# Transposing the second LayerNorm's output by DMA instead of on TensorE in a diffusion transformer block

## Chip, cores and metric

The kernel runs on one core of a Trainium2 chip. The metric is the device time of one execution in microseconds (us). Times inside a trace count from the start of the profiled span, which is about 2 us shorter than the device time. The start of a span scatters by some tenths of a microsecond from run to run, so moments are compared between traces only where the difference is larger than that.

PE is TensorE and PEld its weight load, DVE is VectorE, ACT is ScalarE, POOL is GpSimd. SP issues the loads. ACTq and SPq mark DMA issues on the queues of ACT and SP.

## The reference

One transformer block with adaptive modulation, cut to what matters. There are 512 tokens (B=2, N=256), D=1152, F=4608; all tensors are bfloat16.

```python
mod = (_silu(c) @ w_mod).reshape(B, 6, 1, D)
shift_a, scale_a, gate_a, shift_m, scale_m, gate_m = [mod[:, i] for i in range(6)]
# ... first LayerNorm, qkv, attention with 2 heads ...
x  = x + gate_a * (attention_output @ wo)
h2 = _layernorm(x, axis=-1) * (1 + scale_m) + shift_m     # the part that is changed
m  = _gelu(h2 @ w_fc1) @ w_fc2
return x + gate_m * m
```

## The kernel before

The program is written as a list of units with declared reads and writes. A scheduler orders DVE, ACT and POOL; PE and SP keep the order of the program text. Every wait is a semaphore wait worked out from the reads and writes.

The tokens are handled in four tiles of 128 (t = 0 to 3). For each tile `wo_tile` multiplies by `wo`, adds the residual, and normalises into `XN2[t]`, tokens on the partitions. fc1 needs features on the partitions, so each tile is transposed. Before, PE did that in nine 128x128 pieces into PSUM, and DVE and ACT applied the modulation (scale and shift) while they copied PSUM to `H2T`:

```python
def xn2_T(t):
    ...
    for kt in range(KT):                                  # KT = 9
        tr(slot[kt], xn2[:, kt * 128:(kt + 1) * 128], IDENT)          # PE, into PSUM
    for kt in range(KT):                                  # modulation, PSUM -> H2T
        if kt < (4 if t < 2 else 6): dve(...)             # tensor_scalar, mult and add
        else:                        act(...)             # activation Identity, scale and bias
```

fc1 has 36 output tiles of 128 features. The first F0 of them run in two halves of 256 tokens, so that they can start on token tiles 0 and 1 before 2 and 3 are ready; the others take all 512 tokens. fc1's weights come in nine blocks of 1.18 MB, each for four output tiles, through four buffers: block 4 (for tiles 16 to 19) reuses the buffer of block 0. fc2's weights come in four parts of 2.65 MB. Part 3 lies over the memory of `XN2`, so it has to wait for the last transpose. All these loads are issued by SP, in the order of the text:

```python
# ... wfc1_load(0) to (3) ...
for q4 in range(3):
    dma(WFC2[...], ...)                        # fc2 parts 0, 1, 2: early, ahead of attention's PV
# ... pv(b, h) ...
wo_tile(0); wo_tile(1); wo_tile(2)
xn2_T(0)
wo_tile(3, {2: lambda: xn2_T(1)})              # transposes of tile 1 ahead of the last wo chunk
for f in range(0, 4):        fc1_tile(f, 0, 256)
xn2_T(2)
for f in range(4, F0 - 2):   fc1_tile(f, 0, 256)      # F0 = 8
xn2_T(3)
for f in range(F0 - 2, F0):  fc1_tile(f, 0, 256)
dma(WFC2[:, 27:36, :], ...)                    # fc2 part 3
for f in range(F0):          fc1_tile(f, 256, 256)
for f in range(F0, JT):                        # JT = 36
    if f % 4 == 0 and f // 4 >= 4: wfc1_load(f // 4)
    fc1_tile(f, 0, 512)
# ... fc2, gate, residual, output ...
```

## Time and profile before

| | before |
|---|---|
| device time, median | 249.41 us (249.25 to 249.88) |
| PE busy | 98% of a span of 247.4 us |
| granted TensorE clock | 1.00 throughout |
| start of fc1 tile 16 | about 135.1 us (explained below) |

From the page of the kernel before: the first line gives busy time, share of the span and number of instructions; the rest cut the span into 40 slices of 6.2 us, with PE's busy share and clock in tenths and the DMA rate in GB/s.

```profile
PE 241.7 (98%) x1827; PEld 149.5 (60%) x1827; DVE 69.9 (28%) x179; ACT 63.8 (26%) x129; POOL 19.6 (8%) x33
...
PE   6999999999999999999999999999999999999995
...
PEclk9999999999999999999999999999999999999999
...
GB/s 240 372 375 393 390 299 414 426 423 420 409 385 332 309 364 391 392 386 383 358 156 138 191 191 3 0 0 0 3 16 16 19 16 16 16 19 21 27 19 17
```

PE is the bottleneck and hardly waits. The DMA engines move 299 GB/s or more in slices 2 to 20 and then have less and less to do.

The next lines are PE's part of the timeline of the kernel before: start, duration, engine, line, operation, output and input, count. L681 is the transposes, L678 all other matmuls. Durations overlap a little, because a matmul's end lies after the start of the next.

```profile
96.98 0.67 PE L681 MATMUL psum<-arena 128*128 128x128 bf16 x9
97.48 3.09 PE L678 MATMUL psum<-arena 128*128 128x384 bf16 x18
100.41 0.93 PE L681 MATMUL psum<-arena 128*128 128x128 bf16 x9
101.17 5.55 PE L678 MATMUL psum<-arena 128*128 128x384 bf16 x45
106.56 0.67 PE L681 MATMUL psum<-arena 128*128 128x128 bf16 x9
107.06 2.13 PE L678 MATMUL psum<-arena 128*128 128x256 bf16 x18
109.03 0.74 PE L681 MATMUL psum<-arena 128*128 128x128 bf16 x9
109.60 2.56 PE L678 MATMUL psum<-arena 128*128 128x256 bf16 x22
```

The four transpose groups hold PE from 96.98 to 97.48, 100.41 to 101.17, 106.56 to 107.06 and 109.03 to 109.60: 2.33 us together. That is all that the change can take from PE.

A gelu (L1059) on ACT's timeline of the kernel before tells when an fc1 tile is done. The first whole-width tile is tile 8 (gelu at 121.57), and they follow every 1.944 us.

```profile
135.17 0.60 ACT L1059 ACTIVATE arena<-psum 128x512 bf16<-128x512 f32 x1 [1.34 <-PE psum L678]
```

The gelu at 135.17 is that of tile 15, so PE began tile 16 at about 135.1. What follows it (20 fc1 tiles, fc2, output) takes 112.3 us.

The table by stretches of the kernel before gives, for each stretch, the busy time of each engine, then the granted clock, the DMA engines' busy share and GB/s.

```profile
core 0: us, PE busy (x) PEld busy (x) DVE busy (x) ACT busy (x) POOL busy (x), PEclk, DMA share, GB/s
...
96.00:100.00 4.00, 4.00 (x33) 2.64 (x31) 3.62 (x11) 2.32 (x4) 2.33 (x3) 1.00 1.05 390
100.00:104.00 4.00, 3.91 (x35) 2.83 (x34) 3.88 (x13) 3.45 (x9) 2.72 (x4) 1.00 1.06 392
...
```

While the normalisation and the transposes run, the queue moves fc2's weights at 390 to 392 GB/s.

### The profile page before, as it was taken

Reading aid. Unit: us, or ns where it says so; the run is one execution under the profiler, and the core shown is the slowest. Engines: PE = TensorE matmul, PEld = TensorE weight load, DVE = VectorE, ACT = ScalarE, POOL = GpSimd, SP = SyncE. Lnnn points to the kernel's source line nnn. Section 1 sums busy time; section 2 is a strip of 40 time slices with the busy share of each in tenths; the row PEclk is TensorE's granted clock in tenths of the full one; section 3 lists DMA queues with packets and bytes.
Section 4 is the critical chain, followed back from the end, with each engine's and each line's share of the span. In section 5 each row is a group of like instructions: output and inputs, shape, how many; then the busy total and the mean of one; then the engine's idle time right before and its main releaser. Section 6 shows DMA issues by size and latency. Waiting matters only on the chain.

```text
span 247.4 us, 4146 instructions
## 1 busy us (share of the span) xinstructions
PE 241.7 (98%) x1827; PEld 149.5 (60%) x1827; DVE 69.9 (28%) x179; ACT 63.8 (26%) x129; POOL 19.6 (8%) x33
## 2 busy tenths in 40 slices
PE   6999999999999999999999999999999999999995
PEld 2589954566656766798544444444566666666674
DVE  3742440555322679950000000000012222111112
ACT  4730340344301404984333222332000000000000
POOL 1300000000013167500000000000000000000000
PEclk9999999999999999999999999999999999999999
DMA  6999989999999999999953660000000000000000
GB/s 240 372 375 393 390 299 414 426 423 420 409 385 332 309 364 391 392 386 383 358 156 138 191 191 3 0 0 0 3 16 16 19 16 16 16 19 21 27 19 17
DMA packets 27644, 51.59 MB, mean 209 GB/s; under 512 B 1511, under 2 KB 15591, under 8 KB 26475
## 3 DMA queue, kind: packets, MB, share of 16 engines
q1 hardware_dynamic: 27216, 50.14, 56.0%
q0 software_dynamic: 384, 1.19, 1.5%
q8 instruction: 14, 0.23, 0.4%
q14 instruction: 3, 0.02, 0.0%
q10 hardware_dynamic: 27, 0.00, 0.0%
HBM read 50.14 MB, written 1.19 MB: 208 GB/s over the span
## 4 chain that ended last, share of the span: by engine, by line
PE 94%; ACT 2%; DMA 2%; DVE 1%; issue 0%
PE psum L678 92%; PE psum L681 2%; DMA arena<-in_x_dram 2%; ACT arena L1049 1%; ACT arena L1033 1%; ACT arena L731 1%; ACT arena L730 1%; DVE arena L744 0%; DVE arena L783 0%; DVE arena L1139 0%; DVE arena L732 0%; DVE arena L1140 0%; DVE arena L774 0%; DVE arena L734 0%
## 5 line engine op out<-in xcount | busy, mean ns | idle before, releaser
L678 PE MATMUL psum<-arena 128*128 128x384 bf16 (+7 forms) x1720 | 237.7, 305 | 1.8 <-POOL arena L701 1.4
L678 PEld LDWEIGHTS psum<-arena 128*128 128x128 bf16 (+1 forms) x1720 | 143.8, 97 | 91.0 <-issue 3.1
L1139 DVE TENSOR_TENSOR arena<-psum,arena 128x384 f32<-128x384 f32 (+3 forms) x14 | 7.0, 501 | 119.2 <-PE psum L678 119.2
L1059 ACT ACTIVATE arena<-psum 128x512 bf16<-128x512 f32 (+1 forms) x44 | 22.5, 522 | 42.6 <-PE psum L678 42.6
L673 ACT ACTIVATE arena<-psum 128x512 bf16<-128x512 f32 (+7 forms) x29 | 15.4, 553 | 36.2 <-PE psum L678 33.8
L675 DVE CAST arena<-psum 128x512 bf16<-128x512 f32 (+4 forms) x23 | 14.0, 621 | 32.1 <-PE psum L678 32.0
L1028 POOL TENSOR_TENSOR arena<-arena 128x384 f32<-128x384 f32 x12 | 11.0, 913 | 11.2 <-DVE arena L1027 10.0
L722 DVE BATCH_NORM_STATS2 arena<-arena 128x6 f32<-128x384 f32 (+1 forms) x18 | 9.5, 548 | 0.8 <-DMA arena<-in_x_dram 0.7
L681 PE MATMUL psum<-arena 128*128 128x128 bf16 (+2 forms) x107 | 7.8, 209 | 0.9 <-DMA arena<-in_c_dram 0.7
L681 PEld LDWEIGHTS psum<-arena 128*128 128x128 bf16 (+2 forms) x107 | 6.3, 97 | 3.7 <-DMA arena<-in_c_dram 1.6
L1033 ACT ACTIVATE arena<-arena 128x1152 bf16<-128x1152 f32 x4 | 5.4, 1353 | 9.5 <-DVE arena L1032 9.5
L1027 DVE TENSOR_TENSOR arena<-psum,arena 128x384 f32<-128x384 f32 x12 | 6.6, 548 | 3.2 <-PE psum L678 2.6
L1140 DVE TENSOR_TENSOR arena<-arena 128x384 bf16<-128x384 f32 (+3 forms) x14 | 7.0, 501 | 0.5
L1049 ACT ACTIVATE arena<-psum,arena 128x128 bf16<-128x128 bf16 x16 | 6.1, 460 | 3.2 <-PE psum L681 2.5
L659 POOL DMA_DIRECT2D dit_scratch<-arena x2 | 1.2, 629 | 61.3 <-DVE arena L675 61.3
L1046 DVE TENSOR_SCALAR arena<-psum,arena 128x128 bf16<-128x128 bf16 x20 | 5.5, 338 | 2.0 <-PE psum L681 1.8
L924 ACT ACTIVATE arena<-psum,arena 128x256 bf16<-128x256 f32 x8 | 3.7, 471 | 6.9 <-PE psum L678 5.4
L726 POOL TENSOR_TENSOR arena<-arena 128x1 f32<-128x1 f32 x6 | 3.3, 553 | 8.7 <-DVE arena L725 8.7
L887 ACT ACTIVATE arena<-arena 128x256 bf16<-128x256 bf16 x6 | 2.5, 496 | 4.3 <-DVE arena L881 4.3
L920 DVE TENSOR_REDUCE arena<-psum 128x2 f32<-128x512 f32 x4 | 2.8, 690 | 1.5 <-PE psum L678 1.5
L783 DVE TENSOR_SCALAR arena<-psum,arena 128x256 bf16<-128x256 bf16 x7 | 2.4, 349 | 2.7 <-PE psum L681 1.4
L928 DVE TENSOR_TENSOR arena<-arena 128x512 bf16<-128x512 bf16 x4 | 2.8, 688 | 0.1
(37 smaller groups left out, 30.9 us busy)
## 6 DMA issues: line engine op xcount, KB each, us to landing
arena<-in_w_mod_dram SPq DMA_DIRECT2D x3, 3456.0 KB, 25.9
arena<-in_w_fc_dram SPq DMA_DIRECT2D x9, 1152.0 KB, 8.6
arena<-in_w_fc_dram SPq DMA_DIRECT2D x4, 2592.0 KB, 20.7
arena<-in_wqkv_dram SPq DMA_DIRECT2D x18, 288.0 KB, 10.0
arena<-in_w_mod_dram SPq DMA_DIRECT2D x3, 864.0 KB, 13.1
arena<-in_wqkv_dram SPq DMA_DIRECT2D x1, 2592.0 KB, 10.0
arena<-in_wo_dram SPq DMA_DIRECT2D x1, 2592.0 KB, 39.7
arena<-in_w_mod_dram SPq DMA_DIRECT2D x3, 480.0 KB, 6.8
```

The costliest lines, as they stand in the source:

```text
L673: act(c_act(n), lambda e: e.activation(out=dst, in_=src, func=ACTF.Copy), [src], [dst], name)
L675: dve(c_dve_psum16(n) if psum16 else c_dve_psum32(n), lambda e: e.tensor_copy(dst, src), [src], [dst], name)
L678: S.instr(lambda e: e.matmul(o, lhsT=l, rhs=r, start=st, stop=sp, **kw), reads=[l, r], writes=[o])
L681: S.instr(lambda e: e.transpose(o, i_, idn), reads=[i_, idn], writes=[o])
L722: dve(550, lambda e, s=s, o=o: e.bn_stats(out=o, in_=s), [s], [o], "bn_%s_%d" % (tag, ci))
L1027: dve(550, lambda e, o=o, ga=ga, x1c=x1c: e.tensor_tensor(out=x1c, in0=o, in1=ga, op=ALU.mult), [o, ga], [x1c], "wo_t1_%d_%d" % (t, ci))
L1028: S.op("pool", 930, lambda e, xs=xs, x1c=x1c: e.tensor_tensor(out=x1c, in0=x1c, in1=xs, op=ALU.add), reads=[x1c, xs], writes=[x1c], name=" ...
L1033: act(1344, lambda e: e.activation(out=xn2, in_=x1, func=ACTF.Identity, scale=rs, bias=nm), [x1, rs, nm], [xn2], "xn2_%d" % t)
L1049: act(440, lambda e, o=o, dst=dst, s1=s1, s2=s2: e.activation(out=dst, in_=o, func=ACTF.Identity, scale=s1, bias=s2), [o, s1, s2], [dst], ...
L1059: act(c_act(ntok), lambda e: e.activation(out=dst, in_=o, func=ACTF.Gelu_apprx_tanh), [o], [dst], "gelu_%d_%d" % (f, tok0))
L1139: dve(c_dve_psum32(w), lambda e, o=o, gm=gm, t1=t1: e.tensor_tensor(out=t1, in0=o, in1=gm, op=ALU.mult), [o, gm], [t1], "fc2_t1_%d_%d" % ( ...
L1140: dve(c_dve_32(w), lambda e, t1=t1, x1c=x1c, ost=ost: e.tensor_tensor(out=ost, in0=t1, in1=x1c, op=ALU.add), [t1, x1c], [ost], "fc2_out_%d ...
```

## The change

The intent is to free PE of the transposes. The DMA crossbar transposes `XN2[t]` straight into `H2T`, issued on ACT's queue, and DVE and ACT modulate in place in SBUF. To hide the latency of the transposes of tiles 2 and 3, the first half of fc1 grows from 8 to 12 tiles. To keep the DMA engines free for the transposes, all fc2 loads are issued behind the last one.

```diff
-F0 = 8
+F0 = 12
+        def dma_T(dst, src, nbytes, name):
+            return S.op("act", 100.0, lambda e: e.dma_start_transpose(dst, src), ...)
 # --- in xn2_T(t); tok is the tile's 128 tokens
-            for kt in range(KT):
-                tr(slot[kt], xn2[:, kt * 128:(kt + 1) * 128], IDENT)
-            # modulation from PSUM
+            dma_T(H2T[:, :, tok], XN2[t], P * D * 2, "xn2T_%d" % t)
+            for kt in range(KT):
+                h = H2T[:, kt, tok]
+                if kt % 3 < 2:  dve(... tensor_scalar(out=h, in0=h, ...))     # 6 of 9
+                else:           act(... activation(out=h, in_=h, ...))        # 3 of 9
 # --- order of the program
-        for q4 in range(3):
-            dma(WFC2[part q4], ...)
         # ... pv ...
-        wo_tile(0) ... xn2_T(3), mixed with fc1 tiles as shown above
-        dma(WFC2[part 3], ...)
+        for t in range(4):
+            wo_tile(t)
+            xn2_T(t)
+        for q4 in (3, 0, 1, 2):
+            dma(WFC2[part q4], ...)
+        for f in range(F0):
+            fc1_tile(f, 0, 256)
         for f in range(F0):
             fc1_tile(f, 256, 256)
 # ... (more semaphores for the added DMAs; cut)
```

More of the change, by code (lines that the diff above doesn't have):

```diff
@@ L660, in dma @@
                         name=name, dma_bytes=nbytes * eff, is_out=is_out)
+        def dma_T(dst, src, nbytes, name):
+            return S.op("act", 100.0, lambda e: e.dma_start_transpose(dst, src), reads=[src], writes=[dst], name=name, dma_bytes=nbytes)
         def dve(cost, fn, reads, writes, name):
@@ L1013, in acc_bank, with wo_tile @@
             return b
-        def wo_tile(t, before={}):
+        def wo_tile(t):
             b = t // 2
             for ci in range(NCH):
-                if ci in before:
-                    before[ci]()
                 S.unit("pe", KT * c_mm(CH), "wo_%d_%d" % (t, ci))
@@ L1036, in xn2_T @@
             b = t // 2
-            xn2 = XN2[t]
-            S.unit("pe", KT * c_mm(128), "xn2T_%d" % t)
-            slot = [ps16(7, kt * 128, 128) if kt < 4 else ps16(6, (kt - 4) * 128, 128) for kt in range(KT)]
+            tok = slice(t * 128, (t + 1) * 128)
+            dma_T(H2T[:, :, tok], XN2[t], P * D * 2, "xn2T_%d" % t)
             for kt in range(KT):
-                tr(slot[kt], xn2[:, kt * 128:(kt + 1) * 128], IDENT)
-            for kt in range(KT):
-                o, dst = slot[kt], H2T[:, kt, t * 128:(t + 1) * 128]
+                h = H2T[:, kt, tok]
                 s1, s2 = SC1M[:, kt * 2 + b:kt * 2 + b + 1], SHM[:, kt * 2 + b:kt * 2 + b + 1]
-                if kt < (4 if t < 2 else 6):
-                    dve(335, lambda e, o=o, dst=dst, s1=s1, s2=s2: e.tensor_scalar(out=dst, in0=o, scalar1=s1, scalar2=s2, op0=ALU.mult, op1=ALU.add),
-                        [o, s1, s2], [dst], "h2T_%d_%d" % (t, kt))
-                else:
-                    act(440, lambda e, o=o, dst=dst, s1=s1, s2=s2: e.activation(out=dst, in_=o, func=ACTF.Identity, scale=s1, bias=s2),
-                        [o, s1, s2], [dst], "h2T_%d_%d" % (t, kt))
+                if kt % 3 < 2:
+                    dve(180, lambda e, h=h, s1=s1, s2=s2: e.tensor_scalar(out=h, in0=h, scalar1=s1, scalar2=s2, op0=ALU.mult, op1=ALU.add),
+                        [h, s1, s2], [h], "h2T_%d_%d" % (t, kt))
+                else:
+                    act(440, lambda e, h=h, s1=s1, s2=s2: e.activation(out=h, in_=h, func=ACTF.Identity, scale=s1, bias=s2),
+                        [h, s1, s2], [h], "h2T_%d_%d" % (t, kt))
         def fc1_tile(f, tok0, ntok):
@@ L1098, in build_kernel @@
         wfc1_load(3)
-        for q4 in range(3):
-            dma(WFC2[:, 9 * q4:9 * q4 + 9, :], wfc2_v[:, 9 * q4:9 * q4 + 9, :], 9 * P * D * 2, "ld_wfc2_%d" % q4, run=2304)
         for b in range(2):
@@ L1103, in build_kernel @@
                 pv(b, h)
-        wo_tile(0)
-        wo_tile(1)
-        wo_tile(2)
-        xn2_T(0)
-        wo_tile(3, {2: lambda: xn2_T(1)})
-        for f in range(0, 4):
-            fc1_tile(f, 0, 256)
-        xn2_T(2)
-        for f in range(4, F0 - 2):
-            fc1_tile(f, 0, 256)
-        xn2_T(3)
-        for f in range(F0 - 2, F0):
-            fc1_tile(f, 0, 256)
-        dma(WFC2[:, 27:36, :], wfc2_v[:, 27:36, :], 9 * P * D * 2, "ld_wfc2_3", run=2304)
+        for t in range(4):
+            wo_tile(t)
+            xn2_T(t)
+        for q4 in (3, 0, 1, 2):
+            dma(WFC2[:, 9 * q4:9 * q4 + 9, :], wfc2_v[:, 9 * q4:9 * q4 + 9, :], 9 * P * D * 2, "ld_wfc2_%d" % q4, run=2304)
+        for f in range(F0):
+            fc1_tile(f, 0, 256)
         for f in range(F0):
@@ L1147, in build_kernel @@
             sems = {e: es.enter_context(nc.semaphore("c_" + e)) for e in ENGINES}
-            dma_sems = [es.enter_context(nc.semaphore("d%d" % i)) for i in range(56)]
+            dma_sems = [es.enter_context(nc.semaphore("d%d" % i)) for i in range(64)]
+            S.n_other_dma_sems = 16
             S.emit(nc, block, sems, dma_sems)
```

## The prediction

> **What bounds the kernel now.** TensorE: the page gives PE 241.7 of 247.4 us busy (98%) at granted clock 1.0, and 94% of the chain that ended last. Times below are from the span's start.
>
> **What the change removes.** Four PE groups of nine 128x128 transposes. On the PE timeline, from each group's first transpose to the next matmul: 96.98 to 97.48, 100.41 to 101.17, 106.56 to 107.06, 109.03 to 109.60; in all 2.33 us. That is the largest possible gain (0.9%). Twelve instead of eight fc1 tiles in 256-token halves cost +0.1 us (2x0.984 us against 1.944 us, by the spacing of the gelus).
>
> **What it adds.**
> 1. Each transpose becomes: DMA issue on ScalarE, landing, in-place modulation (six on VectorE, about 0.2 us each, estimated from 0.28 us for 128x256; three on ScalarE, about 0.45 us). The trace has no DMA transpose. The smallest comparable landing is 1.6 us (96 KB output store). The Trainium skill, "VectorE: DVE Perf Modes", The three transpose paths, gives 1309 ns for one 128x128 through the crossbar; a tile here is nine such blocks. I estimate 4 us from issue to landing (2.5 to 6).
> 2. Engine order in the changed build: ScalarE issues transpose 1 only after a modulation that waits for transpose 0; VectorE and ScalarE both stop for transpose 1 before normalisation 2; transposes 2 and 3 are issued after normalisation 3 and three gelus. Before, normalisation 0 ended at 95.74. So: transpose 0 lands about 100, transpose 1 about 105, transpose 3 is issued about 8 us later (113) and lands about 117.
> 3. PE: wo ends about 101.4, the first fc1 tile needs transpose 1, so PE waits about 3.5 us at 101 to 105, perhaps 1 to 2 us more before the second fc1 half.
> 4. The largest cost: all four fc2 loads (10.6 MB) now start behind the last transpose, and the load of fc1 weight block 4 stands behind them on the same queue. The Trainium skill, "DMA: Bandwidth & Descriptors", Queues, rings and completion order, has descriptors consumed in ring order; here queued loads moved at most 390 to 400 GB/s (table by stretches, 104 to 118). 10.6 MB at 392 GB/s is 27 us, block 4 (1.18 MB at about 350 GB/s) 3.4 us, latency about 1.5 us: block 4 lands about 32 us after the last transpose, near 149. Before, fc1 tile 16, its first user, started at about 135.2 (gelus at 121.57 + n x 1.944). The queue idles from about 99 to 117.
>
> **On the critical path.** Tile 16 moves from 135.2 to about 149; the rest (20 fc1 tiles, fc2, output: 112 us) is PE-bound and unchanged, apart from 1 to 2 us if the idle PE loses its clock (not shown by this trace). The saved 2.3 us and the stall at 101 are swallowed by this wait. Sum: 249.4 + 13 = 262 us, range 257 to 270. Faster 1%, within 2% 5%, slower 94%.
>
> **What would show it.** PE idle for about 10 us before fc1 tile 16, released by an fc1 weight load; DMA near zero from about 99 to 117, then full for about 30 us; a shorter PE gap after wo, released by modulations; transposes issue-to-landing near 4 us; fc2 without waits.
>
> **What would make it wrong.** Transposes landing in 2 us or less (about 257), in 6 or more, or blocking ScalarE while issuing (about 270); block 4 not held behind the fc2 loads, which would leave only the wait at 101 (about 250 to 253).

## The result and the profile after

The changed kernel takes 265.43 us (median of 4, 264.33 to 267.33) against 249.64 us (249.25 to 250.16). The ratio is 1.0639, with a 95% interval of 1.0574 to 1.0704. Ratios here are the mean time of one kernel's fast runs over that of the other's of the same rounds, so they are not quite the ratio of the medians quoted.

The page of the changed kernel:

```profile
PE 243.1 (92%) x1818; PEld 152.1 (58%) x1827; DVE 69.9 (27%) x183; ACT 63.6 (24%) x129; POOL 19.6 (7%) x33
...
PE   6999999999999995999990299999999999999995
...
PEclk9999999999999999799998599999999999999999
...
GB/s 248 362 373 394 388 277 419 424 419 421 395 360 264 359 54 59 25 185 399 392 392 383 349 295 182 2 0 0 0 2 29 16 17 15 15 17 15 15 33 16
```

PE has two holes, in slices 16 and 22 to 23, and in or after each of them the clock falls below 9 tenths. The DMA rate falls to 54, 59 and 25 GB/s in slices 15 to 17, just where it was 364 to 392 before, and then is near 390 from slice 19 to 22.

The waits of the changed kernel: who waited for whom, total us, times, longest. L681 is now the matmuls and L1044 DVE's modulation.

```profile
...
PE psum L681 <- DMA arena<-in_w_fc_dram: 11.3, 1, 11.3
...
PE psum L681 <- DVE arena L1044: 3.1, 1, 3.1
...
```

So there are two waits of PE that the kernel before did not have: 3.1 us for a modulation and 11.3 us for an fc1 weight load. The timeline places them. The last column says how long the engine was idle and for what.

```profile
...
96.59 1.32 ACTq L663 DMA_TRANSPOSE arena<-arena  x1
...
99.60 1.35 ACT L1034 ACTIVATE arena<-arena 128x1152 bf16<-128x1152 f32 x1 [3.04 <-DVE arena L1033]
...
100.97 1.32 ACTq L663 DMA_TRANSPOSE arena<-arena  x1
...
104.20 1.26 ACT L1047 ACTIVATE arena<-arena 128x128 bf16<-128x128 bf16 x3 [0.98 <-DMA arena<-arena]
...
105.08 1.42 DVE L1044 TENSOR_SCALAR arena<-arena 128x128 bf16<-128x128 bf16 x6
...
105.43 32.90 PE L681 MATMUL psum<-arena 128*128 128x256 bf16 x251 [3.08 <-DVE arena L1044]
...
111.34 1.36 ACTq L663 DMA_TRANSPOSE arena<-arena  x1
...
114.72 44.70 SPq L659 DMA_DIRECT2D arena<-in_w_fc_dram  x9
...
138.37 0.60 ACT L1057 ACTIVATE arena<-psum 128x512 bf16<-128x512 f32 x1 [1.34 <-PE psum L681]
...
149.60 10.71 PE L681 MATMUL psum<-arena 128*128 128x512 bf16 x41 [11.27 <-DMA arena<-in_w_fc_dram]
149.98 0.15 PEld L681 LDWEIGHTS psum<-arena 128*128 128x128 bf16 x1 [0.27 <-issue]
150.41 0.15 PEld L681 LDWEIGHTS psum<-arena 128*128 128x128 bf16 x1 [0.28 <-issue]
...
```

Tile 0's transpose is issued at 96.59 and tile 1's at 100.97, right after ACT has finished normalising tile 1 (L1034, 99.60 to 100.95). In ACT's order a modulation of tile 0 stands ahead of this issue, but tile 0's transpose had landed at 99.87 by the trace, so waiting for it cost nothing here. PE has finished `wo` at about 102.35 and waits. Tile 1's transpose lands by 104.20, when ACT starts to modulate it; DVE, which has statistics of tile 3 to finish ahead in its order, starts at 105.08, and PE goes on at 105.43. Tile 3's is issued at 111.34 and lands just before 114.72, when SP issues the fc2 loads. Tile 15's gelu is at 138.37, so PE was ready for tile 16 at about 138.3; it began at 149.60, when fc1 block 4 had landed, 34.9 us after SP's issue. PE's own weight loads (PEld) after that stand 0.43 us apart (149.98, 150.41) where nine 512-column matmuls take 1.944 us, 0.216 us each, at full clock.

How long the transposes take, from the summary of their line in the changed kernel (issue to landing, minimum, median, maximum):

```profile
DMA to landing us min/median/max: 3.2/3.3/3.3
```

The table by stretches of the changed kernel shows the queue and the clock:

```profile
...
92.00:96.00 4.00, 4.00 (x26) 2.40 (x25) 3.47 (x8) 0.79 (x1) 2.85 (x5) 1.00 0.15 50
...
104.00:108.00 4.00, 2.57 (x13) 1.69 (x14) 2.65 (x13) 2.56 (x4) 1.62 (x3) 0.61 0.00 0
...
116.00:120.00 4.00, 4.00 (x39) 3.58 (x37) 0.08 (x1) 2.37 (x8) 0.00 (x0) 1.00 0.95 332
120.00:124.00 4.00, 4.00 (x39) 3.59 (x38) 0.00 (x0) 1.61 (x5) 0.00 (x0) 1.00 1.05 399
...
140.00:144.00 4.00, 0.00 (x0) 0.00 (x0) 0.00 (x0) 0.00 (x0) 0.00 (x0) 0.80 1.05 386
144.00:148.00 4.00, 0.00 (x0) 0.00 (x0) 0.00 (x0) 0.00 (x0) 0.00 (x0) 0.50 1.10 350
148.00:152.00 4.00, 2.40 (x6) 0.87 (x7) 0.00 (x0) 0.00 (x0) 0.00 (x0) 0.50 1.10 348
152.00:156.00 4.00, 3.95 (x17) 1.76 (x17) 0.00 (x0) 1.20 (x2) 0.00 (x0) 0.92 1.10 348
...
```

The queue runs empty between 92 and 94, not when the transposes are done but when fc1 blocks 0 to 3 are in. It stays nearly empty for 23 us, which is time for 9 MB at 392 GB/s; then it is full while PE waits.

Tile 16 started at 149.60 in place of 135.1, 14.5 us late. The span grew by 16.1 us (263.5 against 247.4). The other 1.6 us comes after tile 16's start, where the clock is halved.

### The profile page after: what moved, and what is told of

It is laid out like the page before. It is cut to its first block, busy times and chain, and to the rows that moved or that the text cites. A ratio compares the mean times of both kernels' runs of the same rounds, so it can differ in the third digit from the quotient of the medians.

```text
span 263.5 us, 4143 instructions
## 1 busy us (share of the span) xinstructions
PE 243.1 (92%) x1818; PEld 152.1 (58%) x1827; DVE 69.9 (27%) x183; ACT 63.6 (24%) x129; POOL 19.6 (7%) x33
## 4 chain that ended last, share of the span: by engine, by line
PE 86%; DMA 9%; DVE 2%; POOL 1%; issue 0%
PE psum L681 85%; DMA arena<-in_w_fc_dram 8%; PE psum L684 1%; DMA arena<-in_c_dram 1%; DVE arena L1044 1%; POOL arena L1029 1%; DVE arena L1028 1%; DVE arena L725 1%; DVE arena L1033 0%; DVE arena L786 0%; DVE arena L1128 0%; DVE arena L1129 0%; DVE arena L777 0%
## 5 line engine op out<-in xcount | busy, mean ns | idle before, releaser
L681 PE MATMUL psum<-arena 128*128 128x384 bf16 (+7 forms) x1747 | 241.0, 305 | 16.6 <-DMA arena<-in_w_fc_dram 11.3
L681 PEld LDWEIGHTS psum<-arena 128*128 128x128 bf16 (+1 forms) x1756 | 148.4, 98 | 105.1 <-issue 17.7
L1057 ACT ACTIVATE arena<-psum 128x256 bf16<-128x256 f32 (+1 forms) x48 | 23.0, 490 | 55.1 <-PE psum L681 55.1
L676 ACT ACTIVATE arena<-psum 128x512 bf16<-128x512 f32 (+7 forms) x29 | 15.4, 553 | 37.3 <-PE psum L681 34.8
L1034 ACT ACTIVATE arena<-arena 128x1152 bf16<-128x1152 f32 x4 | 5.4, 1345 | 13.8 <-DVE arena L1033 13.8
L1044 DVE TENSOR_SCALAR arena<-arena 128x128 bf16<-128x128 bf16 x24 | 6.0, 324 | 5.6 <-DMA arena<-arena 5.6
L684 PEld LDWEIGHTS psum<-arena 128*128 128x128 bf16 (+2 forms) x71 | 4.1, 97 | 3.1 <-DMA arena<-in_c_dram 1.6
L684 PE MATMUL psum<-arena 128*128 128x128 bf16 (+2 forms) x71 | 4.9, 204 | 0.7 <-DMA arena<-in_c_dram 0.7
L1047 ACT ACTIVATE arena<-arena 128x128 bf16<-128x128 bf16 x12 | 5.0, 484 | 2.0 <-issue 1.0
## 6 DMA issues: line engine op xcount, KB each, us to landing
arena<-in_w_mod_dram SPq DMA_DIRECT2D x3, 864.0 KB, 12.9
```

The costliest lines, as they stand in the source:

```text
L676: act(c_act(n), lambda e: e.activation(out=dst, in_=src, func=ACTF.Copy), [src], [dst], name)
L681: S.instr(lambda e: e.matmul(o, lhsT=l, rhs=r, start=st, stop=sp, **kw), reads=[l, r], writes=[o])
L684: S.instr(lambda e: e.transpose(o, i_, idn), reads=[i_, idn], writes=[o])
L1034: act(1344, lambda e: e.activation(out=xn2, in_=x1, func=ACTF.Identity, scale=rs, bias=nm), [x1, rs, nm], [xn2], "xn2_%d" % t)
L1044: dve(180, lambda e, h=h, s1=s1, s2=s2: e.tensor_scalar(out=h, in0=h, scalar1=s1, scalar2=s2, op0=ALU.mult, op1=ALU.add), [h, s1, s2], [h] ...
L1057: act(c_act(ntok), lambda e: e.activation(out=dst, in_=o, func=ACTF.Gelu_apprx_tanh), [o], [dst], "gelu_%d_%d" % (f, tok0))
```

## Experiments

The main theory (A): the loss is the order of the loads. fc1 block 4 stands on the same queue behind 10.6 MB of fc2 weights, which cannot start before the last transpose. The rival (B): the loss is the transposes themselves, that is their latency, their issue on ACT, and the modulation in place. The medians of the kernel before, on the same chips in the same rounds, were 249.5 to 249.8 us.

### e1: the order of the loads alone

```diff
-        for q4 in (3, 0, 1, 2): wfc2_load(q4)        # behind the last transpose
+        wfc2_load(3); wfc2_load(0)                   # behind the last transpose
         # ... fc1 tiles in halves ...
+        wfc1_load(4); wfc2_load(1); wfc1_load(5); wfc1_load(6); wfc2_load(2)
-        # wfc1_load(4), (5), (6) each ahead of its first tile
```

> The changed kernel with only the order of loads on the queue altered: still everything behind the last transpose, but fc1 blocks 4, 5 and 6 are put between the fc2 loads (fc2 part 3, 0, block 4, part 1, blocks 5 and 6, part 2, ...). Theory A (the loss is block 4 standing behind 10.6 MB of fc2 weights): the wait of 11.3 us before fc1 tile 16 and the half clock after it go away, tile 16 starts near 138.3 in place of 149.6, total about 252.9 us (before 249.6 plus the 3.2 us by which tile 16 would still be late). Theory B (the loss comes from the transposes, their issue on ScalarE or their in-place modulation): the total stays above 260 us.

Measured: 252.51 us (251.45 to 253.22), ratio 1.0107 (1.0078 to 1.0136). The order of instructions on PE, DVE, ACT and POOL was the same as in the changed kernel, as far as the two traces record it (on ACT one gelu and one transpose issue, which start within 0.06 us of each other, are swapped). PE's waits between 95 and 180:

```profile
...
PE psum L681 <- DVE arena L1044: 3.1, 1, 3.1
...
```

The wait for the load is gone and only the 3.1 us remain. Of the 15.8 us that the change costs, 12.9 us (265.43 less 252.51) is the order of the loads. Theory A holds for that part; about 2.7 us is left for B.

### e2: fc2 parts 0 to 2 early again, the transposes beside them

```diff
+        for q4 in range(3): wfc2_load(q4)            # ahead of pv, as in the kernel before
         # ... wo, transposes ...
-        for q4 in (3, 0, 1, 2): wfc2_load(q4)
+        wfc2_load(3)
```

> The changed kernel with fc2 parts 0, 1 and 2 loaded early as before the change, so that the transposes run beside full-rate loads; part 3 stays behind the last transpose. If crossbar transposes share the DMA engines well (landing stays at 3.3 to 4 us): about 253 us, as e1. If each 256-byte transpose descriptor has to alternate with a 2304-byte load packet of about 95 ns (74 per engine, so about 7 us more at worst): transposes land in 8 to 10 us, the wait after wo grows from 3.1 to 10 us or more, total 260 us or more; then the postponed loads were needed by the transposes.

Measured: 264.11 us (262.96 to 265.76), ratio 1.0580. Block 4 is now in time, but PE waits 14.1 us at another place. The waits between 95 and 120, and the landing of the transposes:

```profile
...
PE psum L681 <- DVE arena L1044: 14.1, 1, 14.1
...
```

```profile
DMA to landing us min/median/max: 3.2/5.0/12.7
```

Transpose 0 took 12.7 us to land and transpose 1 6.8 us (issued at 108.58, first modulated at 115.37), against 3.3 us on a quiet queue; the two later ones, issued when the loads had ended, took about 3.2 us again. The trace's packet records show why. A transpose is 1152 packets of 256 bytes and 32 tiny ones. Alone they run at up to some 840 per microsecond, and one transpose is through in 1.55 us. Beside the loads, 152 to 160 went through per microsecond from 101 to 107, and in each of these microseconds nearly the same number of load packets of 2304 bytes (149 to 158). The two queues thus got equal numbers of packets, as if they took turns, and the small packets were held to the pace of the large ones. (The records do not name the DMA engine, so the order on one engine is not shown.) The first packet also came later: 4.0 us after the issue, against 1.2 us on the quiet queue. The postponed loads were thus not a needless part of the change: simply taking them back costs as much as it gains.

### e3: late fc2 loads in the kernel before

```diff
-        for q4 in range(3): dma(WFC2[part q4], ...)  # early
         # ... xn2_T(3), still on PE ...
+        for q4 in (3, 0, 1, 2): dma(WFC2[part q4], ...)
-        dma(WFC2[part 3], ...)
```

> The kernel before, with PE transposes and F0 = 8, and only the fc2 loads moved: all four behind the last transpose group, in the order 3, 0, 1, 2. Theory A: SP issues at about 109.7, block 4 lands 34.8 us later as in the changed kernel, near 144.5, tile 16 is 9.4 us late, plus about 1.7 us of half clock: about 260.7 us. Theory B: near 249.6 us, within 2 us.

Measured: 261.00 us (260.17 to 261.39), ratio 1.0446 (1.0425 to 1.0468). PE waited between 95 and 180 for the load:

```profile
...
PE psum L678 <- DMA arena<-in_w_fc_dram: 9.3, 1, 9.3
...
```

Without any DMA transpose, the late loads alone cost 11.2 us. That is the second, independent showing of theory A. It is less than in the changed kernel because PE's transposes are done sooner, and the loads start sooner with them: SP issues them at 109.81 in this trace, against 114.72.

### e4: the wait for block 4 filled with dummy matmuls

```diff
         if f == 16:
+            for i in range(50): mm(ps32(7), IDENT, Q4B, True, True)   # unused PSUM bank
```

> The changed kernel with 50 dummy matmuls of 512 columns into an unused PSUM bank (10.8 us at full clock) before fc1 tile 16, so that PE does not go idle in the wait for block 4. If the half clock after the wait costs what its eight slow matmuls show (427 against 216 ns, about 1.7 us), the total falls from 265.4 to about 263.7 us, with granted clock 1.00 from 140 to 153. If the clock is not set by the idle time, no change.

Measured: 264.30 us (262.50 to 265.17), ratio 1.0567. The dummy matmuls change no output. The table by stretches, for comparison with the changed kernel's from 140 on:

```profile
...
144.00:148.00 4.00, 4.00 (x20) 1.84 (x19) 0.00 (x0) 0.00 (x0) 0.00 (x0) 1.00 1.10 349
148.00:152.00 4.00, 3.85 (x19) 1.59 (x17) 0.00 (x0) 0.60 (x1) 0.00 (x0) 1.00 1.10 348
...
```

The clock is 1.00 in these stretches, and by the trace's clock record from 108.5 to 262.1. From the start of tile 16 to the last output arithmetic on DVE the trace has 109.6 us against 111.1 us in the changed kernel. So the halved clock was caused by PE's idleness and cost 1.5 us. The medians differ by only 1.1 us; both kernels scatter by 3 us, so the smaller figure contradicts nothing.

### e8: twelve fc1 tiles in halves, in the kernel before

```diff
-F0 = 8
+F0 = 12
```

> The kernel before with F0 = 12 in place of 8 and nothing else: two halves cost 1.968 us against 1.944 for a whole tile, four tiles 0.1 us: 249.9 us, ratio 1.000 to 1.001. A ratio above 1.004 would mean that the halves cost more than their matmul spacing says.

Measured: 249.98 us (249.40 to 250.11), ratio 1.0007 (0.9994 to 1.0019). The halves cost nothing that can be told from zero.

### e5, e6 and e7: fewer transposes by DMA, and the first gap filled

e5 and e6 send only some tiles through the crossbar, all with the order of loads of e1. Tiles 2 and 3 have the first half of fc1 to hide behind. Tile 1 is the one that PE waits for, so it stays on PE.

```diff
 # e5                                            # e6
         wo_tile(0); wo_tile(1); wo_tile(2)       wo_tile(0)
         xn2_T(0)                           # PE  xn2_T_dma(0)
                                                  wo_tile(1); wo_tile(2)
         wo_tile(3, {2: xn2_T(1)})          # PE  wo_tile(3, {2: xn2_T(1)})      # PE
+        xn2_T_dma(2); xn2_T_dma(3)               xn2_T_dma(2); xn2_T_dma(3)
 # e7: e1, and between wo_tile(3) and the first fc1 tile
+        for i in range(12): mm(ps32(7), IDENT, Q4B, True, True)
```

> Only token tiles 2 and 3 go through the crossbar, which have the first half of fc1 (11.8 us) to hide behind; tiles 0 and 1 stay on PE as before; 12 tiles in halves; loads in the order of e1, none beside a transpose. If the transposes cost only where PE waits for them: the two removed PE groups (0.50 and 0.57 us) are gained, 0.1 us is lost on the halves, total about 248.8 us against 249.8 (ratio 0.996), no PE wait from 95 to 180. If the ScalarE issue or the in-place modulations hurt by themselves (gelus late, second half of fc1 late): 250 us or more.

> As e5, with tile 0 through the crossbar as well; tile 1, the one that PE waits for, stays on PE. Expected another 0.5 us less than e5, about 248.3 us, if VectorE's stop for transpose 0 does not delay the evacuations of wo and the transposes of tile 1; up to 250 us if it does, to be seen as a PE wait before tile 1's transposes or the first fc1 tile.

> e1 with 12 dummy matmuls (2.6 us) in the gap of 3.1 us after wo. The wait for tile 1's modulation stays, the half clock after it (granted 0.68 from 104 to 108) goes: about 1.3 us less than e1, so about 251.2 us, with clock 1.000 in all runs. If the low clock has another cause, 252.5 us as e1.

Measured: e5 251.74 us (250.47 to 253.09), ratio 1.0087; e6 251.96 us (250.54 to 253.21), ratio 1.0096; e7 252.87 us (252.55 to 253.31), ratio 1.0134. All three missed what was expected, by 1.7 to 3.7 us. e5's waits between 95 and 180 say why:

```profile
...
PE psum L681 <- DMA arena<-in_w_fc_dram: 2.0, 1, 2.0
...
```

This is the fault of the experiments' own order of loads. e1 put block 5 behind fc2 part 1. In e1 PE came to tile 20 late enough not to notice; as soon as the first gap was made shorter, PE came earlier and waited 2.0 us (e5) or 1.7 us (e7). The scatter has a second part. The three runs of e5 with a mean clock of 0.999 to 1.000 took 250.5 to 251.0 us, and the three with 0.993 took 252.4 to 253.1. The profiled run of e6 has the lower clock, and its table by stretches has 0.74 from 144 to 148 and 0.84 from 148 to 152, right after its wait of 2.2 us for block 5. The other slow runs of e5 and e6 were not profiled; by their mean clocks, a wait of about 2 us sometimes brings a spell of half clock and sometimes not.

### e9, e10 and e11: the same with the loads in the order of need

```diff
-        wfc2_load(3); wfc2_load(0)
+        wfc2_load(3)
         # ... fc1 tiles in halves ...
-        wfc1_load(4); wfc2_load(1); wfc1_load(5); wfc1_load(6); wfc2_load(2)
+        wfc1_load(4); wfc1_load(5); wfc2_load(0); wfc1_load(6); wfc2_load(1)
         # at tile 16: wfc1_load(7), wfc2_load(2); at tile 20: wfc1_load(8)
```

> e5 waited 2.0 us before fc1 tile 20, because its own order of loads put block 5 behind fc2 part 1; here blocks 4 and 5 come directly behind fc2 part 3, and each later block ahead of the next fc2 part. If that was all that e5 lost: no PE wait after 95, clock 1.000 in all runs, about 248.7 us, ratio 0.996. If the crossbar path costs something else as well: above 249.6 us.

> e6 with the same mended order. Expected 248.2 to 248.6 us: half a microsecond less PE work than e9, against which stands a wait of about 0.5 us of tile 1's transposes for their normalisation, which e6 showed. Equal to e9 if that wait is as long as the removed group.

> e7 (all four tiles through the crossbar, gap after wo filled with dummy matmuls) with the mended order. e7 waited 1.7 us for block 5, so about 251.2 us here (ratio 1.006), with clock 1.000: what is left over 249.6 is then the gap of 3.1 us after wo plus 0.1 for the halves, less the removed transposes. If e7's missing gain had another cause than block 5, about 252.8 us.

Measured: e9 248.85 us (248.75 to 249.04), ratio 0.9973 (0.9961 to 0.9986). e10 248.34 us (248.02 to 248.59), ratio 0.9948 (0.9933 to 0.9962). e11 251.13 us (250.70 to 251.49), ratio 1.0062 (1.0048 to 1.0077). All as expected. The differences of e9 and e10 are small but clear of the noise.

e10 beats both kernels, if only by half a percent. Its chain of work that ended last shows PE without a break from 101.47 on (start, us, what):

```profile
...
101.47 142.30 PE psum L681 x945
...
```

e11 has all four tiles on the crossbar, as in the change, and no half clock (1.000 in every run). Against e1 it is 1.4 us faster by the medians; the one run of e1 with full clock, at 251.45 us, is close to it, so this is about what the clock cost after the first gap. e11 remains 1.5 us slower than the kernel before. Its trace accounts for nearly all of that. From the first dummy matmul (102.09) to the first fc1 matmul (105.34) are 3.25 us, and the first nine fc1 matmuls, which each need another modulated piece of tile 1, take 0.37 us longer than at their later spacing of 0.109 us. With 0.1 us for the halves and less the 2.33 us of freed PE time this is 1.4 us.

In e5 to e7 and e9 to e11 one or two of the late transposes took 4.3 to 4.9 us to land, although no loads ran beside them. In each of these cases a 16 KB packet that fetches instructions, about 1 us long, fell among the transposes' packets; in the changed kernel it came after the last transpose, and all four took 3.2 to 3.3 us. That the fetch is the cause was not tested.

### e12: e9 with early fc2 loads

```diff
+        for q4 in range(3): wfc2_load(q4)            # ahead of pv
         # ... the later wfc2_load(0), (1), (2) taken out
```

> e9 with fc2 parts 0 to 2 loaded early, so that transposes 2 and 3 run beside full-rate loads. In e2 a loaded queue let through about 155 transpose descriptors per microsecond, one for each load packet. Both transposes have 2368: issued at about 107 and 108.6, they land near 122 to 124 in place of 113, the second half of fc1 starts about 9 us late, total 257 to 260 us. If e2's slow transposes had another cause (tile 0 alone, or VectorE waiting for it): about 249 us.

Measured: 252.44 us (252.33 to 253.57), ratio 1.0126. The direction was right (3.6 us slower than e9), the size was not. PE's waits and ACT's timeline in this run:

```profile
...
PE psum L681 <- DVE arena L1063: 1.6, 1, 1.6
PE psum L681 <- ACT arena L1076: 1.2, 1, 1.2
...
```

```profile
...
107.45 1.84 ACTq L663 DMA_TRANSPOSE arena<-arena  x1
...
109.34 4.72 ACTq L663 DMA_TRANSPOSE arena<-arena  x1
114.11 1.49 ACT L1076 ACTIVATE arena<-psum 128x256 bf16<-128x256 f32 x5 [5.01 <-PE psum L681]
...
```

The expectation had the loads last past 120. They were issued from 81 on and ran out between 111 and 114 (377 GB/s from 111 to 112, 122 GB/s from 113 to 114). The first transpose packet moved at 111.50, 4.0 us after the issue, as in e2, so the transposes met only the tail of the loads: they landed after 9.1 and 8.1 us, the first at about 116.6. One thing was not expected at all: the second issue held ACT's queue for 4.72 us, the gelus stopped for 5.0 us, and PE waited 1.2 us for their PSUM banks besides 1.6 us for the modulation.

## Why the prediction was right

1. **The gain.** The removed PE work was put at no more than 2.33 us. e9 realised 0.8 us of the 1.07 us of two groups, and e10 1.3 us of 1.57. This held.
2. **The cost of the load order.** It was put at 13.8 us (tile 16 from 135.2 to 149) and measured as 14.5 us (135.1 to 149.60). The mechanism is shown twice, by e1 and e3. The prediction rested on the Trainium skill, "DMA: Bandwidth & Descriptors", Queues, rings and completion order, by which descriptors are consumed in ring order. The runs agree: block 4 landed 34.8 us after the fc2 issue when it was last in the row, and in time when it was moved up.
3. **The size of its terms.** Two terms were off and nearly cancelled, which was luck. The last transpose was put at 117 and was in at 114.6: tile 1's landed 0.8 us earlier than predicted, the issue of the last followed 7.2 us after that and not 8, and it landed in 3.3 us, not 4. Block 4 was to land 32 us after it and took 34.8. The packet records show where the added 2.8 us lie. As many bytes as the four fc2 parts and block 4 hold together (11.8 MB) had been moved at 147.0, 32.3 us after the issue, as predicted. But when block 4 had landed, at 149.47, it was 12.65 MB: 0.86 MB of the blocks behind it, 2.5 us at 349 GB/s, had moved before its last bytes. The queue ran empty between 92 and 94, not at 99.
4. **The first gap.** PE was to wait 3.5 us behind wo; it waited 3.1. One reason given for it did not bind: ACT issued transpose 1 behind a modulation that waits for transpose 0, as predicted, but the normalisation of tile 1, done at 100.95, came later than that landing (99.87) and set the issue. In the changed kernel it stands ahead of the longer wait for block 4, which sets the time whenever PE arrives; e1 and e11 show the first gap's own cost once block 4 is in time.
5. **The second gap.** One to two more microseconds "perhaps" before the second half of fc1 did not appear: after 105.43 PE went on without a wait to tile 16.
6. **The clock.** "1 to 2 us if the idle PE loses its clock" was left out of the sum of 262; it did happen, and cost 1.5 us by e4. That, the 0.7 us in point 2, and the 0.8 us by which the sum had rounded 13.8 down to 13 are 3.0 of the 3.4 us between 262 and 265.4. The Trainium skill, "TensorE: Matmul & The Clock Gate", What's actually happening, says that an idle window of about 3.4 us halves the clock and a busy one restores it. The trace agrees for the long wait: granted clock 0.50 from 144 to 152 after the 11.3 us wait, and 1.00 again about 3 us after PE resumed. Its spells of half clock last 3.41 us and 10.24 us, one and three times 3.41. For short gaps it does not agree: after the first gap, of 3.1 us and so shorter than the window, the clock was halved here too, and e1 lost its clock in three runs of four (0.993) and not in the fourth (1.000, 251.45 us). What decides in such a gap is not shown.

What "would make it wrong" was told apart by the runs too: with block 4 no longer held behind fc2, the prediction said 250 to 253 us, and e1 gave 252.51.

So where did the expected gain of the change go? It was at most 2.3 us. A wait for the transposes' round trip, which PE-side transposes do not have, eats it (e11: 1.5 us slower in all). And the loads that were moved to make room for the transposes turned into a much longer wait, one stage later, of a load that nobody had moved.

## What to carry to other kernels

Moving a load also moves everything behind it on its queue: before postponing one, list what stands behind it and when each is first needed, and let the loads follow the order of need. A DMA transpose is free for the engine that it relieves only where other work covers its landing (3.2 to 4.9 us here on a queue without loads) and its modulation; use it for those tiles and keep the tile that the engine waits for where it was. Keep bulk loads away from it: beside them its packets went through at a fifth of their rate alone (e2). The best kernel here, e10, still leaves the queue empty of loads from 94 to 114; what it mended is the order of the loads behind. Whether that time can be used for loads between the transposes was not tried.

## What the Trainium skill lacked or had wrong

- "DMA: Bandwidth & Descriptors" (its rules say that a transpose next to ordinary DMAs needs nothing, which is about correctness) does not say what such a transpose costs in time. It does describe that an engine serves its queues in turn, packet by packet, and the equal counts in e2 fit that; the cost is what is missing: beside a full load queue a transpose landed in 12.7 us in place of 3.3 (e2), its first packet came 4.0 us after the issue in place of 1.2, and then about 155 of its 256-byte packets went through per microsecond, beside as many 2304-byte load packets, against up to some 840 alone.
- "Advanced Engine Details and Errata", X-Bar Transpose (TRN2), has transposes "as fast as regular DMAs" and expects 350 to 400 GB/s. From SBUF to SBUF, 128x1152 bfloat16 took 1.55 us of packets on a quiet queue, which is 190 GB/s (294,912 bytes), where plain loads moved 392 GB/s. Larger transposes were not tried.
- "VectorE: DVE Perf Modes", The three transpose paths, gives 1309 ns for one 128x128 block through the crossbar. Nine blocks in one transfer took 3.3 us from issue to landing, so the figure can't be multiplied by the number of blocks; packets moved in 1.55 us of the 3.3.
- "Perfetto Trace Analysis", DMA Instruction — HWDGE, describes that the issuing sequencer is held while descriptors are made, but gives no time for a transpose (the DMA page has sequencer cycles of earlier generations, in its part on trn3 and for other shapes). Here it was 1.3 us on a quiet queue, 1.9 us beside loads in e2, and 1.84 and 4.72 us in e12, where the loads were running out; during the longest one ACT's gelus stopped.
- "TensorE: Matmul & The Clock Gate" was right about the clock after a long wait. Its explanation asks for an idle window of about 3.4 us, and its rules for authors warn of gaps over about 3 us. Here a gap of 3.1 us cost the clock in three runs of four (e1), and shorter gaps can too: in e6 the profiled run had half clock for 3.4 us after a gap of 2.2 us, and in e5, with a gap of 2.0 us, three runs of six had the lower clock.
